# Contracting 128 rows instead of 64 in the products of a head's last key tile

## The chip, the cores and the metric

The kernel runs on one core of a Trainium2 chip. The metric is the device time of one execution in microseconds (us); of several executions the median is given. A profile is of one execution. TensorE (PE) multiplies: it loads a block of weights (PEld, up to 128 rows by 128 columns) and streams a moving operand through it; the rows are the ones that a product contracts. VectorE (DVE), ScalarE (ACT) and GpSimd (POOL) do the rest, SyncE (SP) issues most transfers. Each engine takes its instructions in order.

## The reference

64 heads (8 batches of 8) of causal attention with a decay, 576 positions of 64 values each, and then a two-layer network over the 4608 rows:

```python
scores = scale * np.matmul(q, k.transpose(0, 1, 3, 2))      # 64 heads, 576 x 576
cum = np.cumsum(np.log(np.clip(f, 0.0001, 1.0)), axis=-1)
scores = np.where(causal, -1000000000.0, scores + cum[:, :, :, None] - cum[:, :, None, :])
attn = np.exp(scores - np.max(scores, axis=-1, keepdims=True))
attn = attn / (np.sum(attn, axis=-1, keepdims=True) + 1e-09)
x = np.matmul(attn, v)                                      # -> 4608 x 512
h = np.maximum(x @ w_in, 0.0)                               # 512 -> 2048
out = h * h @ w_out                                         # 2048 -> 512
```

## The kernel before

Scores are computed transposed: keys lie on partitions and queries along the free axis, so that the exponentials `p` of a key tile are directly the moving operand of the product with V ("AV"). The 576 keys make five key tiles, four of 128 and a last one of 64 (`KT`; `kn` is a tile's number of keys). `UNITS` lists the six units of a head as (key tile, first query, end of queries): tile 0 for queries 256 to 576, tiles 2, 3, 4 and 1, and tile 0 for the queries below 256. Unit 3 is the last key tile: 64 keys by 64 queries. V comes from memory with 640 rows, of which the last 64 are zero.

There are two kinds of heads. The first 14 (`NWHOLE`, "whole" heads) use float32 as it is, which PE takes in two passes. In them the causal mask of a diagonal block is a product of its own behind the score product: the matrix `mz` (whose last 128 columns hold -1e9 above the diagonal) times a unit matrix `eye`, both bfloat16, accumulated on the scores (lines 346 and 348). Their AV is one product of V with `p` (line 411). The other 50 ("split" heads) split each operand into a high and a low part: two score products (lines 352 and 355), the exponential on ACT into `p` (362), the mask as an affine select on POOL (364), a cast of `p` to the high part `ph` on ACT (377), the low part `pl` by a subtraction on DVE (378), and three AV products, low times high, high times low, high times high (388, 389, 390), 65 columns of weights wide with a column of ones for the denominator (64 in the middle one).

The work is laid out in slots, one for each unit of each head. A slot emits the score and exponential of its unit (`score`), the AV products of the unit two slots back (`LAG`), and then what tables put there: loads, the preparation of later heads, row maxima (a product at line 313, a reduction on DVE at 319, a small transfer that writes the maxima into a row of the score's operand), and divisions. A split head's cast and subtraction follow in the next slot at the latest (`split_last`). In the first slots the weights are converted (DVE, ACT, and a subtraction on POOL at 210); when eight heads are done, the network's products (line 477 for the first layer, 500 for the second) fill in between (`fill`). The order of tracing is the order on PE, ACT, DVE and POOL (`in_order`); tile pools and semaphores do the rest. The buffers of `p` rotate: two in the split heads, three each for odd and even units in the whole heads (they share the names `ph` and `pl`).

Of the kernel before, what the change touches and what calls it, by code (L numbers as in the profile page):

```python
# [9 lines left out]
F32 = mybir.dt.float32  # L10
# [4 lines left out]
ALU = mybir.AluOpType  # L15
# [18 lines left out]
def decay_attention_relu2_kernel(  # L34
# [18 lines left out]
    nc = tc.nc  # L53

    NH, D, _, S = qk.shape
    P = 2 * D
    H = 8
    B = NH // H
    NJ = v.shape[2]
# [22 lines left out]
    def bank(use):  # L82

        turn = banks[use] or banks["s"]
        b = turn.pop(0)
        turn.append(b)
        return psum.tile([P, 512], F32, name=f"bank{b}")


    MW = 448  # L90
    mz = cpool.tile([P, MW], BF16, name="mz")
    nc.gpsimd.memset(mz, 0.0)
    nc.gpsimd.affine_select(
        out=mz[:, MW - P:], in_=mz[:, MW - P:], pattern=[[-1, P]],
# [3 lines left out]
    eye = wk.tile([P, 448], F32, name="p").bitcast(BF16)[:, :P]  # L98
    nc.gpsimd.memset(eye, 0.0)
    nc.gpsimd.affine_select(  # L100
        out=eye, in_=eye, pattern=[[-1, P]],
# [124 lines left out]
    KT = [(j * P, min(P, S - j * P)) for j in range(NJ)]  # L226
# [110 lines left out]
    def score(h, u):  # L337
        st = state[h]
        j, q0, q1 = UNITS[u]
        k0, kn = KT[j]  # L340
        n = q1 - q0
        ps = bank("s")
        if h < NWHOLE:
            masked = q0 == k0
            r, k = st["whole"][:, 0], st["whole"][:, 1]
            nc.tensor.matmul(ps[:kn, :n], k[:, k0:k0 + kn], r[:, q0:q1], start=True, stop=not masked)
            if masked:
                nc.tensor.matmul(
                    ps[:kn, :kn], mz[:kn, MW - P:MW - P + kn], eye[:kn, :kn], start=False, stop=True,
                )  # L350
        else:
            nc.tensor.matmul(  # L352
                ps[:kn, :n], st["kl0"][:D + 3, k0:k0 + kn], st["r2"][:D + 3, q0:q1], start=True, stop=False,
            )
            nc.tensor.matmul(  # L355
                ps[:kn, :n], st["l2"][:, k0:k0 + kn], st["r1"][:, q0:q1], start=False, stop=True,
            )
        if h < NWHOLE:
            p = wk.tile([P, 448], F32, name=("ph", "pl")[u % 2], bufs=3)
        else:  # L360
            p = wk.tile([P, 448], F32, name="p")
        nc.scalar.activation(out=p[:kn, :n], in_=ps[:kn, :n], func=AF.Exp, scale=SCALE)  # L362
        if h >= NWHOLE and q0 == k0:
            nc.gpsimd.affine_select(  # L364
                out=p[:kn, :kn], in_=p[:kn, :kn], pattern=[[1, kn]],
                compare_op=ALU.is_ge, fill=0.0, base=0, channel_multiplier=-1,
            )
        st["p"][u] = p

    def split_p(h, u):  # L370
        st = state[h]
        j, q0, q1 = UNITS[u]
        kn, n = KT[j][1], q1 - q0
        p = st["p"][u]
        ph = wk.tile([P, 448], F32R, name="ph", bufs=3)
        pl = wk.tile([P, 448], F32R, name="pl", bufs=3)
        nc.scalar.copy(out=ph[:kn, :n], in_=p[:kn, :n])  # L377
        nc.vector.tensor_tensor(  # L378
            out=pl[:kn, :n], in0=p[:kn, :n], in1=ph[:kn, :n].bitcast(F32), op=ALU.subtract,
        )  # L380
        st["p"][u] = ph, pl

    def av_split(st, acc, u, o, i, first, last):
        j = UNITS[u][0]
        kn = KT[j][1]
        ph, pl = st["p"][u]
        vh, vl = st["vh"][:kn, j, :D + 1], st["vl"][:kn, j, :]
        nc.tensor.matmul(acc[:D + 1, o], vh, pl[:kn, i], start=first, stop=False)  # L388
        nc.tensor.matmul(acc[:D, o], vl, ph[:kn, i], start=False, stop=False)  # L389
        nc.tensor.matmul(acc[:D + 1, o], vh, ph[:kn, i], start=False, stop=last)  # L390

    def av_part(h, u, low):

        j, q0, q1 = UNITS[u]
        s0, s1 = (q0, min(q1, QA)) if low else (max(q0, QA), q1)
        if s0 >= s1:
            return
        st = state[h]
        first = u == (NU - 1 if low else 0)
        last = u == NU - 2  # L400
        if first:
            st["av"] = bank("av")
        acc = st["av"]
        kn = KT[j][1]
        base = 0 if low else QA
        o, i = slice(s0 - base, s1 - base), slice(s0 - q0, s1 - q0)
        if h < NWHOLE:

            vr = st["vr"].rearrange("p j d -> p (j d)")
            vr = vr[:kn, j * (D + 2):min(j * (D + 2) + P, NJ * (D + 2))]  # L410
            nc.tensor.matmul(acc[:vr.shape[1], o], vr, st["p"][u][:kn, i], start=first, stop=last)
        else:
            av_split(st, acc, u, o, i, first, last)
        if last:
            n = QA if low else S - QA
            if not low:
                if h % H == 0:
                    xts[h // H] = wk.tile([P, NCC, S], F32, name=f"xt{h // H % 2}", bufs=1)
                if h % 2 == 0:
                    st["den"] = wk.tile([P, S], F32, name="den")  # L420
                else:
                    st["den"] = state[h - 1]["den"]
            o = (h % 2) * D
            x = xts[h // H][o:o + D, (h % H) // 2, base:base + n]
            nc.scalar.copy(out=x, in_=acc[:D, :n])
            nc.scalar.copy(out=st["den"][o:o + 1, base:base + n], in_=acc[D:D + 1, :n])  # L426
# [136 lines left out]
    def split_last():  # L563
        while unsplit:
            split_p(*unsplit.pop())
# [79 lines left out]
    for n in range(-2 * NU, last_slot + 1):  # L645
        live = 0 <= n < len(slots)
        split_last()
        if live:
            h, u = slots[n]
            score(h, u)  # L650
            if h >= NWHOLE:
                unsplit.append((h, u))
        for ha, ua in avs.get(n, ()):
            if ua < NU - 1:
                av_part(ha, ua, False)
            else:
                av_part(ha, ua, True)
                av_part(ha, ua - 1, True)
        for args in fins.get(n, ()):
            finish(*args)  # L660
        for do in events.get((n, 0), ()):
            do()
        wr = RATES[0 if n < -NU else 1 if n < 0 else 2 if n < NA else 3]
        cv(wr / 2)
        fill(n, 0.5)
        for do in events.get((n, 1), ()):
            do()
        cv(wr / 2)
        fill(n, 1.0)
# [44 lines left out]
```

## Time and profile before

| | |
|---|---|
| median of 3 runs | 1255.66 us (1254.82 to 1255.89) |
| the profiled execution | 1255.36 us |
| its span, first to last instruction | 1253.3 us |
| granted clock of PE, mean | 0.995 |
| busy: PE, PEld, DVE, ACT, POOL | 1193.5, 1051.8, 785.1, 702.0, 372.4 us |
| HBM read, written | 60.20, 9.88 MB |
| products of 64 rows: line 348, line 411, lines 388 to 390 | 14, 28, 3 x 50 |

Busy times overlap: a PE product counts from its start until its modelled end, and the next starts meanwhile. The distance between two starts tells what a product costs in a chain. In the rows, `64*65` behind a product is the number of rows and columns of its weights, and `64x64` the partitions and elements of the moving operand; float32 rows may stand for the rounded type too. An arrow `<-` behind a time names what ended the wait.

### The profile page before, as it was taken

What the parts mean: (1) busy time and instruction counts of PE and PEld (TensorE: products, weight loads), DVE (VectorE), ACT (ScalarE), POOL (GpSimd) and SP (SyncE); (2) the same over time, 40 slices, a digit from 0 to 9 for tenths busy, and PEclk for the clock granted to TensorE, in tenths of its full rate; (3) what the DMA queues carried; (4) which work ended last, traced back from release to release, by engine and by line L of the source; (5) the groups of instructions that cost most, each with busy time, mean ns of one, the idle gap of its engine ahead of it and who ended that gap; (6) DMA issues with size and microseconds to landing.
All of it is one profiled execution on the core that took longest, in us unless ns stands there. A gap on an engine that the chain in (4) does not pass through costs nothing.

```text
span 1253.3 us, 23182 instructions
## 1 busy us (share of the span) xinstructions
PE 1193.5 (95%) x7652; PEld 1051.8 (84%) x7652; DVE 785.1 (63%) x2042; ACT 702.0 (56%) x1720; POOL 372.4 (30%) x512
## 2 busy tenths in 40 slices
PE   3877899999999999999999999999999999999998
PEld 2544687888989899999899989998998989999997
DVE  7658776666666767666656566667665766532332
ACT  3545455556666666665565556666666666632332
POOL 4323223333333333333322233334333333200000
PEclk9999999999999999999999999999999999999999
DMA  8857631112121112121201121211121212000000
GB/s 199 193 129 176 177 87 26 51 32 57 41 55 33 48 37 57 40 57 26 55 18 52 31 57 32 55 34 52 40 57 41 57 41 52 17 27 1 18 18 17
DMA packets 115639, 71.90 MB, mean 57 GB/s; under 512 B 97384, under 2 KB 97384, under 8 KB 115520
## 3 DMA queue, kind: packets, MB, share of 16 engines
q1 hardware_dynamic: 114400, 66.30, 21.7%
q0 software_dynamic: 1120, 4.13, 1.5%
q8 instruction: 61, 1.00, 0.3%
q14 instruction: 58, 0.48, 0.1%
HBM read 60.20 MB, written 9.88 MB: 56 GB/s over the span
## 4 chain that ended last, share of the span: by engine, by line
PE 63%; ACT 1%; issue 1%; POOL 1%; DMA 0%; DVE 0%; SPq 0%; POOLq 0%; DVEq 0%; ACTq 0%
PE bank L477 25%; PE bank L500 24%; PE bank L388 3%; PE bank L355 2%; PE bank L390 2%; PE bank L389 2%; PE bank L313 2%; PE bank L352 2%; DMA den<-rdr 0%; ACT ph L377 0%; ACT den L426 0%; ACT r L485 0%; ACT p L362 0%; POOL v L299 0%; ACT rl L281 0%
## 5 line engine op out<-in xcount | busy, mean ns | idle before, releaser
L500 PE MATMUL bank<-w,gh 128*128 128x512 f32 x1152 | 413.8, 400 | 0.0
L477 PE MATMUL bank<-xh,w 128*128 128x256 f32 x2304 | 330.7, 286 | 4.9 <-DVE tcol L319 4.9
L378 DVE TENSOR_TENSOR pl<-p,ph 128x320 fp32r<-128x320 f32 (+4 forms) x300 | 186.9, 623 | 206.6 <-ACT ph L377 197.1
L477 PEld LDWEIGHTS bank<-xh,w 128*128 128x128 f32 x2304 | 301.2, 190 | 13.8 <-DVE tcol L319 5.3
L500 PEld LDWEIGHTS bank<-w,gh 128*128 128x128 f32 x1152 | 217.6, 189 | 39.0
L485 ACT ACTIVATE r<-bank 128x256 f32<-128x256 f32 x288 | 110.4, 383 | 211.7 <-PE bank L477 198.3
L500 PE MATMUL bank<-w,gl 128*128 128x512 f32 x576 | 227.1, 394 | 0.2 <-DVE gl L488 0.2
L486 DVE TENSOR_TENSOR g<-r 128x256 f32<-128x256 f32 x288 | 127.3, 442 | 144.2 <-ACT r L485 143.4
L364 POOL TENSOR_SCALAR_AFFINE_SELECT p<-p 128x128 f32<-128x128 f32 (+1 forms) x250 | 81.5, 326 | 454.2 <-ACT p L362 313.5
L377 ACT CAST ph<-p 128x320 fp32r<-128x320 f32 (+4 forms) x300 | 124.4, 415 | 148.9 <-POOL p L364 147.1
L477 PE MATMUL bank<-xl,w 128*128 128x256 f32 x1152 | 185.3, 283 | 0.0
L319 DVE CUSTOM_DVE_ANT_0 bank<-bank,mz 128x256 f32<-128x256 f32 (+4 forms) x320 | 133.7, 432 | 45.9 <-PE bank L313 44.5
L477 PEld LDWEIGHTS bank<-xl,w 128*128 128x128 f32 x1152 | 158.9, 191 | 0.0
L362 ACT ACTIVATE p<-bank 128x320 f32<-128x320 f32 (+4 forms) x300 | 115.8, 386 | 71.7 <-PE bank L355 67.3
L488 DVE TENSOR_TENSOR gl<-g,gh 128x256 fp32r<-128x256 f32 x288 | 128.9, 448 | 35.7 <-ACT p L362 0.9
L313 PE MATMUL bank<-rk 66*128 66x320 f32 (+9 forms) x384 | 111.8, 318 | 24.8 <-DMA rk<-qkraw 13.4
L487 ACT ACTIVATE gh<-r 128x256 fp32r<-128x256 f32 x288 | 120.5, 418 | 9.1
L500 PEld LDWEIGHTS bank<-w,gl 128*128 128x128 f32 x576 | 109.3, 190 | 14.3 <-DVE gl L488 0.9
L313 PEld LDWEIGHTS bank<-rk 66*128 66x128 f32 (+3 forms) x384 | 68.7, 185 | 40.1 <-DVE tcol L319 17.1
L388 PE MATMUL bank<-pl,vh 128*65 128x320 f32 (+4 forms) x350 | 99.4, 284 | 1.6 <-ACT den L426 1.4
L389 PE MATMUL bank<-ph,v 128*64 128x320 f32 (+4 forms) x350 | 94.8, 271 | 0.0
L390 PE MATMUL bank<-ph,vh 128*65 128x320 f32 (+4 forms) x350 | 93.0, 271 | 0.0
(71 smaller groups left out, 1498.2 us busy)
## 6 DMA issues: line engine op xcount, KB each, us to landing
qkraw<-in_qk SPq DMA_DIRECT2D x50, 288.0 KB
v<-in_v SPq DMA_DIRECT2D x64, 160.0 KB
den<-rdr SPq DMA_DIRECT2D x64, 144.0 KB
out<-osb SPq DMA_DIRECT2D x36, 256.0 KB
w<-in_w_in SPq DMA_DIRECT2D x16, 512.0 KB
w<-in_w_out SPq DMA_DIRECT2D x16, 512.0 KB
rl<-in_qk SPq DMA_DIRECT2D x14, 288.0 KB
rk<-in_qk POOLq DMA_DIRECT2D x14, 288.0 KB, 4.7
```

What stands on the lines that cost most here:

```text
L313: nc.tensor.matmul(ps[:m, :n], st["r2"][:rows, q0:q0 + m], st["kl0"][:rows, k0:k0 + n], start=True, stop=True,)
L319: nc.vector.tensor_tensor_reduce(out=ps[:m, :n], in0=ps[:m, :n], in1=mz[:m, mo:mo + n], op0=ALU.add, op1=ALU.min, scale=-1.0, scalar=init, ...
L377: nc.scalar.copy(out=ph[:kn, :n], in_=p[:kn, :n])
L378: nc.vector.tensor_tensor(out=pl[:kn, :n], in0=p[:kn, :n], in1=ph[:kn, :n].bitcast(F32), op=ALU.subtract,)
L388: nc.tensor.matmul(acc[:D + 1, o], vh, pl[:kn, i], start=first, stop=False)
L389: nc.tensor.matmul(acc[:D, o], vl, ph[:kn, i], start=False, stop=False)
L390: nc.tensor.matmul(acc[:D + 1, o], vh, ph[:kn, i], start=False, stop=last)
L477: nc.tensor.matmul(ph[:, :T], w[:, s, cc], x[:, cc, :], start=(cc == 0 and k == 0), stop=(cc == NCC - 1 and k == 2),)
L486: nc.vector.tensor_tensor(out=g, in0=r, in1=r, op=ALU.mult)
L487: nc.scalar.activation(out=gh, in_=r, func=AF.Square)
L488: nc.vector.tensor_tensor(out=gl, in0=g, in1=gh.bitcast(F32), op=ALU.subtract)
L500: nc.tensor.matmul(po, g[:, ts], w[:, s], start=(fc == 0 and k == 0), stop=(fc == NF - 1 and k == 2),)
```

## The change

Where the last key tile's operands have 64 partitions, the change uses all 128. The mask product takes all rows of `mz` and `eye`, whose rows 64 to 127 are zero in the columns used. Partitions 64 to 127 of the exponentials' buffer are cleared on POOL, while the exponential goes on writing 0 to 63; the cast and the subtraction run over all 128 partitions; and the AV products contract 128 rows, in which the rows of keys that don't exist are zero in `p`, `ph`, `pl` and V. Units of full key tiles are as before, and the score products keep their shape.

```diff
-                    ps[:kn, :kn], mz[:kn, MW - P:MW - P + kn], eye[:kn, :kn], start=False, stop=True,
+                    ps[:kn, :kn], mz[:, MW - P:MW - P + kn], eye[:, :kn], start=False, stop=True,
...
+        if kn < P:
+
+            nc.gpsimd.memset(p[kn:, :n], 0.0)
         nc.scalar.activation(out=p[:kn, :n], in_=ps[:kn, :n], func=AF.Exp, scale=SCALE)
...
-        nc.scalar.copy(out=ph[:kn, :n], in_=p[:kn, :n])
+        nc.scalar.copy(out=ph[:, :n], in_=p[:, :n])
         nc.vector.tensor_tensor(
-            out=pl[:kn, :n], in0=p[:kn, :n], in1=ph[:kn, :n].bitcast(F32), op=ALU.subtract,
+            out=pl[:, :n], in0=p[:, :n], in1=ph[:, :n].bitcast(F32), op=ALU.subtract,
         )
...
-        vh, vl = st["vh"][:kn, j, :D + 1], st["vl"][:kn, j, :]
-        nc.tensor.matmul(acc[:D + 1, o], vh, pl[:kn, i], start=first, stop=False)
-        nc.tensor.matmul(acc[:D, o], vl, ph[:kn, i], start=False, stop=False)
-        nc.tensor.matmul(acc[:D + 1, o], vh, ph[:kn, i], start=False, stop=last)
+        vh, vl = st["vh"][:, j, :D + 1], st["vl"][:, j, :]
+        nc.tensor.matmul(acc[:D + 1, o], vh, pl[:, i], start=first, stop=False)
+        nc.tensor.matmul(acc[:D, o], vl, ph[:, i], start=False, stop=False)
+        nc.tensor.matmul(acc[:D + 1, o], vh, ph[:, i], start=False, stop=last)
...
-            vr = vr[:kn, j * (D + 2):min(j * (D + 2) + P, NJ * (D + 2))]
-            nc.tensor.matmul(acc[:vr.shape[1], o], vr, st["p"][u][:kn, i], start=first, stop=last)
+            vr = vr[:, j * (D + 2):min(j * (D + 2) + P, NJ * (D + 2))]
+            nc.tensor.matmul(acc[:vr.shape[1], o], vr, st["p"][u][:, i], start=first, stop=last)
```

On PE, ACT and DVE no instruction is added or moved; PE's keep their order, and only the row counts change, which the listed order does not tell. On POOL 64 memsets come in. In a split head it stands ahead of the affine select of the same tile. POOL before, in the middle of the split heads (brackets: the engines and queues whose semaphores an instruction waits for):

```order
L364 AFFINE_SELECT p<-p 128x128 [waits Activation_49]
L364 AFFINE_SELECT p<-p 64x64 [waits Activation_49]
L290 TENSOR_TENSOR rl<-qkraw,rl 64x576 [waits Pool_49]
L364 AFFINE_SELECT p<-p 128x128 [waits DVE_49,Activation_49,Pool_49]
L299 TENSOR_TENSOR v<-v,vh_80 128x320 [waits DMAHW7_49,DVE_49,PE_49]
```

And with the change (three lines came in above, so that line 364 is now the memset and 367 the select):

```order
L367 AFFINE_SELECT p<-p 128x128 [waits Activation_49]
L364 MEMSET p 64x64 [waits DVE_49,Pool_49]
L367 AFFINE_SELECT p<-p 64x64 [waits Activation_49]
L290 TENSOR_TENSOR rl<-qkraw,rl 64x576
L367 AFFINE_SELECT p<-p 128x128 [waits DVE_49,Activation_49,Pool_49]
```

One instruction came in, with a wait for DVE, which reads the buffer's earlier content; the rest kept its order. In a whole head the memset stands behind POOL's part in the weights (`w`, line 210) and ahead of a later head's load (252). POOL with the change, in the first whole heads:

```order
L268 MEMSET v 128x5x2
L210 TENSOR_TENSOR w_250<-osb,w_250 128x512 [waits DMAHW6_49,Activation_49]
L364 MEMSET pl 64x64 [waits Pool_49]
L252 DMA rk_77<-in_qk 64x1152 [waits DMASW1_49,PE_49]
L210 TENSOR_TENSOR w_302<-osb,w_302 128x512 [waits DMAHW7_49,Activation_49,Pool_49]
```

On ACT the exponential of the last tile in the whole heads (from the second head on) waits for POOL too. Before:

```order
L426 COPY den<-bank_309 1x256
L362 ACTIVATE ph<-bank_323 128x192 [waits PE_49,Activation_49]
L181 ACTIVATE wmag<-w_193 128x512 [waits DMAHW0_49,DVE_49]
L362 ACTIVATE pl<-bank_345 64x64 [waits PE_49,Activation_49]
L362 ACTIVATE ph<-bank_354 128x448 [waits PE_49,Activation_49]
```

And with the change:

```order
L427 COPY den<-bank_310 1x256
L365 ACTIVATE ph<-bank_324 128x192 [waits PE_49,Activation_49]
L181 ACTIVATE wmag<-w_193 128x512 [waits DMAHW0_49,DVE_49]
L365 ACTIVATE pl<-bank_346 64x64 [waits PE_49,Activation_49,Pool_49]
L365 ACTIVATE ph<-bank_356 128x448 [waits PE_49,Activation_49]
```

Nothing moved there; the fourth row has one wait more. In the split heads the exponential has no such wait.

More of the change, by code (lines that the diff above doesn't have):

```diff
@@ L372, in split_p @@
         j, q0, q1 = UNITS[u]
-        kn, n = KT[j][1], q1 - q0
+        n = q1 - q0
         p = st["p"][u]
@@ L384, in av_split @@
         j = UNITS[u][0]
-        kn = KT[j][1]
         ph, pl = st["p"][u]
-        vh, vl = st["vh"][:kn, j, :D + 1], st["vl"][:kn, j, :]
-        nc.tensor.matmul(acc[:D + 1, o], vh, pl[:kn, i], start=first, stop=False)
-        nc.tensor.matmul(acc[:D, o], vl, ph[:kn, i], start=False, stop=False)
-        nc.tensor.matmul(acc[:D + 1, o], vh, ph[:kn, i], start=False, stop=last)
+        vh, vl = st["vh"][:, j, :D + 1], st["vl"][:, j, :]
+        nc.tensor.matmul(acc[:D + 1, o], vh, pl[:, i], start=first, stop=False)
+        nc.tensor.matmul(acc[:D, o], vl, ph[:, i], start=False, stop=False)
+        nc.tensor.matmul(acc[:D + 1, o], vh, ph[:, i], start=False, stop=last)
     def av_part(h, u, low):
@@ L403, in av_part @@
         acc = st["av"]
-        kn = KT[j][1]
         base = 0 if low else QA
```

## The prediction

> **What bounds the kernel now.** I began with the head of the page, then asked for the busy time of each engine by stage.
>
> ```profile
> span 1253.3 us, 23182 instructions
> PE 1193.5 (95%) x7652; PEld 1051.8 (84%) x7652; DVE 785.1 (63%) x2042; ACT 702.0 (56%) x1720; POOL 372.4 (30%) x512
> ```
>
> ```profile
> 31.00:62.00 31.00, 25.28 (x124) 17.71 (x123) 19.11 (x57) 18.15 (x45) 9.89 (x14) 1.00 0.84 194
> 125.00:157.00 32.00, 26.17 (x137) 20.99 (x136) 24.03 (x49) 14.56 (x35) 8.85 (x11) 0.91 0.65 175
> 157.00:188.00 31.00, 30.35 (x182) 25.19 (x181) 22.95 (x57) 16.02 (x39) 8.17 (x8) 1.00 0.33 87
> ...
> 220.00:1110.00 890.00, 884.05 (x5917) 798.34 (x5916) 584.89 (x1562) 548.98 (x1367) 300.31 (x423) 1.00 0.18 44
> ```
>
> The columns are the stretch, its length, and the busy time (with instruction count) of PE, PEld, DVE, ACT and POOL, then granted clock, DMA share and GB/s. There are two regimes. Up to about 157 us PE is busy for only 25 to 26 us of each 31 or 32 while the DMA engines are 65 to 84% busy: loads and the conversion of the weights hold the pace. From there on PE is busy almost without a break, 884.05 of 890 us in the stretch that holds the 50 split heads, with the clock at 1.00. No other engine is above 66% there. The waits of PE in that stretch, longest first, confirm it:
>
> ```profile
> PE bank L313 <- DVE tcol L319: 3.4, 3, 1.6
> PE bank L388 <- ACT den L426: 1.4, 4, 0.4
> ```
>
> The longest wait group is 3.4 us in 890. So in this stretch what PE spends is what the kernel spends, and a busy PE is not yet a PE at its peak: a product's recorded time includes its latency. What a product costs is the distance from its start to the next start, and that is in the timeline. Here is PE around the last key tile's three AV products of one split head (columns: start, duration, engine, line, operation and tiles, rows*columns of the weights, shape of the moving operand):
>
> ```profile
> 578.92 0.28 PE L355 MATMUL bank<-rl 128*128 128x256 f32 x1
> 579.13 0.24 PE L388 MATMUL bank<-pl,vh 64*65 64x64 f32 x1
> 579.21 0.22 PE L389 MATMUL bank<-ph,v 64*64 64x64 f32 x1
> 579.27 0.22 PE L390 MATMUL bank<-ph,vh 64*65 64x64 f32 x1
> ...
> 580.47 0.40 PE L477 MATMUL bank<-xl,w 128*128 128x256 f32 x2
> ```
>
> And the same lines for a full key tile, in the same head's neighbourhood, contracting 128 rows and followed by the same MLP products:
>
> ```profile
> 586.43 0.28 PE L390 MATMUL bank<-ph,vh 128*65 128x256 f32 x1
> 586.55 0.22 PE L388 MATMUL bank<-pl,vh 128*65 128x128 f32 x1
> 586.61 0.22 PE L389 MATMUL bank<-ph,v 128*64 128x128 f32 x1
> 586.67 0.22 PE L390 MATMUL bank<-ph,vh 128*65 128x128 f32 x1
> ...
> 587.73 0.64 PE L477 MATMUL bank<-xl,w 128*128 128x256 f32 x4
> ```
>
> A product with a 256-wide moving operand passes on after 0.12 us (586.43 to 586.55), but before the 64-row product 0.21 us go by (578.92 to 579.13): 0.09 us lost on entry. From the last product of the trio to the first xl product of the MLP take 1.06 us with 128 rows (586.67 to 587.73) and 1.20 us with 64 rows (579.27 to 580.47), though the latter moves half as many columns: 0.14 us lost on exit. So the path into and out of a 64-row product is not pipelined. Is it the rows, or that everything here is 64 wide? This kernel has narrow products with more than 64 rows:
>
> ```profile
> 593.50 0.20 PE L352 MATMUL bank<-rk 67*64 67x64 f32 x1
> 593.53 0.22 PE L355 MATMUL bank<-rl 128*64 128x64 f32 x1
> 593.59 0.34 PE L388 MATMUL bank<-pl,vh 128*65 128x320 f32 x1
> ...
> 597.82 0.20 PE L313 MATMUL bank<-rk 66*64 66x64 f32 x1
> ...
> 598.88 0.64 PE L477 MATMUL bank<-xl,w 128*128 128x256 f32 x4
> ```
>
> With 64 columns of weights and 64 moving columns, but 67 and 128 rows, the steps are 0.03 and 0.06 us, and from a 66-row one to the xl product again 1.06 us (597.82 to 598.88). Rows of 66 or 67 lose nothing, rows of 64 do. The gap belongs to the contraction of 64 rows.
>
> **The change part by part.**
>
> *AV of the last tile, split heads.* Three products per head go from 64 to 128 rows; their number and their moving columns stay.
>
> ```profile
> L388 PE MATMUL bank<-pl,vh 64*65 64x64 f32 x50 | 12.1, 242 | 0.0
> ```
>
> Fifty heads, one trio each. Before, from the start of the product ahead to the first xl product: 580.47 - 578.92 = 1.55 us. After, two bounds. By the 128-wide trio: 0.12 + 0.06 + 0.06 + 1.06 = 1.30 us, saving 0.25. By the narrow products at their shortest step: 0.12 + 0.03 + 0.03 + 1.06 = 1.24 us, saving 0.31. The second narrow product above is already followed after 0.06 us, as though the next weights set the step, so I stay close to the first: 0.26 us, 50 x 0.26 = 13.0 us. Should one of the two ends keep its gap, about 0.1 to 0.15 us a head would be left; nothing in the 128-row rows speaks for that. A loss on PE is excluded by the same rows: no product of these lines with 128 rows starts later than its neighbour's columns ask.
>
> The Trainium skill's page "TensorE: Matmul & The Clock Gate", section "Why this matters for your kernels", says that a single product with 32 rows takes the same time as one with 128. By that rule every term on PE would be zero and the kernel's time 1255.4 us; the rows above, 1.20 us against 1.06 us behind products of 64 and 66 rows, disagree for products in a chain with others.
>
> *Mask product and AV in the 14 whole heads.* Here the mask product contracts 64 rows and then 128, and the AV product (two passes) likewise:
>
> ```profile
> 98.56 0.33 PE L346 MATMUL bank<-rl 128*64 128x64 f32 x2
> 98.82 0.21 PE L348 MATMUL bank<-p,mz 64*64 64x64 bf16 x1
> 98.96 0.81 PE L411 MATMUL bank<-pl,v 128*128 128x320 f32 x2
> ...
> 100.35 0.22 PE L348 MATMUL bank<-p,mz 128*128 128x128 bf16 x1
> 100.41 0.54 PE L411 MATMUL bank<-ph,v 128*128 128x192 f32 x2
> ...
> 101.22 0.22 PE L348 MATMUL bank<-p,mz 128*128 128x128 bf16 x1
> 101.37 0.33 PE L411 MATMUL bank<-pl,v 64*66 64x64 f32 x2
> ```
>
> A 128-row mask passes on after 0.06 us (100.35 to 100.41); a 64-row mask after 0.14 (98.82 to 98.96), and into a 64-row AV product it takes 0.15 (101.22 to 101.37). So an end costs 0.08 to 0.09 us again, and each of the two 64-row places of a whole head has two ends: some 0.2 us for each, 0.4 us a head (estimate, from the split trio's 0.23 at its two ends). Whether that counts depends on the regime.
>
> ```profile
> L348 PE MATMUL bank<-p,mz 64*64 64x64 bf16 x3 | 0.6, 213 | 0.0
> ```
>
> Three such masks lie between 157 and 220 us, where PE is the bound: 3 x 0.4 = 1.2 us. The other 11 heads are worth 11 x 0.4 = 4.4 us on PE, in a stage where PE idles a fifth of the time. Both ends are open: nothing, if loads and weights alone hold the pace, or all of it, if the idle time only follows PE's own order. PE's idle share there is near the first, so I take a quarter: 1.1 us.
>
> *The added memset.* POOL clears 64x64 values 64 times. Nearest rows:
>
> ```profile
> L268 POOL MEMSET v<- 128x10 f32 x14 | 1.8, 125 | 0.0
> L117 POOL MEMSET rl<- 64x576 f32 x2 | 1.1, 574 | 0.1
> ```
>
> Ten values per partition cost 125 ns, 576 cost 574; interpolated, 64 cost about 170 ns, with these two as ends. 64 of them are 11 us of POOL, which is 30% busy. In a split head the memset stands between two affine selects on POOL, and what it could delay is the second one (behind the exponential of the same tile), then the cast and the subtraction, then the AV products two slots on. Around one:
>
> ```profile
> 568.51 0.29 POOL L364 TENSOR_SCALAR_AFFINE_SELECT p<-p 128x128 f32<-128x128 f32 x1 [1.93 <-ACT p L362]
> 571.79 0.22 ACT L362 ACTIVATE p<-bank 64x64 f32<-64x64 f32 x1 [0.82 <-PE bank L355]
> ```
>
> POOL is free at 568.80 and the exponential starts only at 571.79, because PE's scores come late: 3 us of cover for 0.17 us. The memset's wait for the buffer's last reader (DVE) is one that the exponential has already. I put it at nothing; without the cover it would delay one tile's select by 0.17 us. In the whole heads the exponential itself gains a wait for the memset (13 of 14), and there POOL can be late:
>
> ```profile
> 98.59 1.27 POOL L210 TENSOR_TENSOR w<-osb,w 128x512 fp32r<-128x512 f32 x1 [5.33 <-ACT w L209]
> 99.80 0.11 POOL L268 MEMSET v<- 128x10 f32 x1
> 99.13 0.22 ACT L362 ACTIVATE pl<-bank 64x64 f32<-64x64 f32 x1 [0.61 <-PE bank L348]
> 100.75 0.68 ACT L181 ACTIVATE wmag<-w 128x512 f32<-128x512 f32 x1 [1.40 <-DVE osb L197]
> ```
>
> Here the memset could start at 99.91 and the exponential at about 100.1 instead of 99.13, 0.95 us late. It would end by 100.3, ahead of its reader at 101.37, and ACT's next work comes at 100.75. Behind the memset POOL's queue holds the load of a later head, which would go out 0.17 us later. Cost: nothing here, and zero to 1 us over the stage; I take zero.
>
> *The wider cast and subtraction* work on 128 partitions instead of 64 with the same 64 columns. Elements per partition don't change; no price.
>
> *What is late next.* DVE and ACT have a third of their time free, so a head that is 0.26 us shorter (of some 17.8: 890 us over 50 heads) leaves them cover; still, some small waits will grow where PE arrives earlier. I take back 5% of 13.0, 0.6 us.
>
> Sum: 13.0 + 1.2 + 1.1 - 0.6 = 14.7 us. The profiled execution took 1255.36 us (span 1253.3), 0.3 us below the median of 1255.66. 1255.36 - 14.7 = 1240.7 against its own time; against the median 1241.0.
>
> **The rivals.**
>
> *The time is given back as waits.* Each product of the next head needs maxima from DVE and a bank that ACT has emptied, and the two wait rows above show that PE already touches both. If half of the 13.0 us turned into such waits, and the early heads gave nothing, the time would be 1255.7 - 6.5 - 0.6 = 1248.6 us. Against it: those waits total under 5 us now and the engines are at two thirds. 1 in 10.
>
> *The early heads give all.* If PE's order holds the first stage as well, 4.4 us come instead of 1.1, and with 0.31 us a trio the time would be 1255.7 - 15.5 - 1.2 - 4.4 = 1234.6 us. PE's 25 of 31 us leave it possible: 1 in 12.
>
> *No change.* If the gap comes from something that these 64-column products share and rows don't touch, 1255.7 us. The 66- and 67-row products speak against it: 3 in 100. The page's rule named above would end here too.
>
> *Slower: ACT behind POOL in the whole heads.* The new wait makes ACT, which issues in order, stand behind POOL's weight subtractions (L210, 1.27 us) when it comes to the last tile's exponential. If all 13 heads lost 1.27 + 0.17 = 1.4 us and all of that reached PE, 18.7 us would be lost against 14.7 won: 1259.7 us. It decides from about 1.1 us a head reaching PE. In the case above 0.95 us would arise and be absorbed. 3 in 100.
>
> **How the numbers follow.** The forecast holds 3 of 4 chances, 1241.0 us. Its own range runs from 1255.7 - 15.5 - 1.2 - 2 = 1237 to 1255.7 - 12.5 + 1.8 = 1245 (0.25 us a head, nothing from the early heads, 1.8 us of new waits or of ACT's delay). The range for 8 in 10 reaches into the two neighbouring rivals, 1236 to 1247; outside lie no change, slower, and the far parts of these two. A measurement of this kernel can tell 0.2% (2.5 us) from no change. All but no change and slower make it faster by more than that: faster 0.93, same 0.04, slower 0.03 (a little of the first rival's tail goes to same).
>
> **What would show it.** In the timeline after, the trio should start 0.12 us behind the score product, step by 0.03 to 0.06, and the distance from its first neighbour to the first xl product should be 1.24 to 1.30 us in place of 1.55. The split heads' stretch should shrink by 12 to 15 us, the stretch before 157 us by at most 4. POOL should show 64 memsets near 170 ns, with no exponential waiting on POOL in the split heads. PE's waits for DVE and ACT should stay under 8 us between 220 us and the last head. The prediction is wrong if the 128-row trio keeps either gap, if PE's idle time grows by about what the gaps gave, or if ACT's waits for POOL in the whole heads appear as PE idle time.

## The result, and the profile after

| | before | changed |
|---|---|---|
| median of 4 runs | 1255.24 us (1254.28 to 1255.89) | 1242.68 us (1241.21 to 1245.07) |
| ratio | | 0.9902, 95% interval 0.9879 to 0.9925 |
| the profiled execution | 1255.36 us | 1241.21 us |

Faster by 12.6 us; 14.7 were forecast, as 1241.0 us in 1236 to 1247. Run again beside the experiments, twice, the changed kernel stood at 0.9905 (0.9886 to 0.9924) and 0.9897 (0.9878 to 0.9916). The first rows to read are again the stretches of the changed kernel (length, then busy time of PE, PEld, DVE, ACT and POOL, clock, DMA share, GB/s):

```profile
31.00:62.00 31.00, 24.07 (x123) 17.12 (x121) 18.80 (x56) 17.83 (x44) 10.55 (x17) 1.00 0.85 181
125.00:157.00 32.00, 27.45 (x149) 22.93 (x148) 23.91 (x51) 14.90 (x36) 8.80 (x10) 0.86 0.61 164
220.00:1110.00 890.00, 882.97 (x5994) 804.12 (x5993) 589.64 (x1576) 551.84 (x1375) 308.25 (x472) 1.00 0.18 44
```

Busy time hardly tells of the change: PE's 882.97 us of 890 were 884.05 before. What has changed is how many products fit in, 5994 for 5917. The distances in the timeline of the changed kernel tell why (start, duration, engine, line, weights as rows*columns, moving operand):

```profile
571.85 0.28 PE L355 MATMUL bank<-rl 128*128 128x256 f32 x1
571.97 0.19 PE L390 MATMUL bank<-pl,vh 128*65 128x64 f32 x1
572.00 0.22 PE L391 MATMUL bank<-ph,v 128*64 128x64 f32 x1
572.06 0.22 PE L392 MATMUL bank<-ph,vh 128*65 128x64 f32 x1
572.12 1.20 PE L478 MATMUL bank<-xh,w 128*128 128x256 f32 x8
573.15 0.40 PE L478 MATMUL bank<-xl,w 128*128 128x256 f32 x2
```

The first of the trio now starts 0.12 us behind the score product (0.21 before), the next ones after 0.03 and 0.06, and the xl product comes at 1.30 us (1.55 before). Over 49 heads the median of that distance fell from 1553 to 1300 ns. The whole heads show it too:

```profile
98.43 0.33 PE L346 MATMUL bank<-rl 128*64 128x64 f32 x2
98.59 0.19 PE L348 MATMUL bank<-p,mz 128*64 128x64 bf16 x1
98.71 0.81 PE L412 MATMUL bank<-pl,v 128*128 128x320 f32 x2
...
100.98 0.22 PE L348 MATMUL bank<-p,mz 128*128 128x128 bf16 x1
101.03 0.28 PE L412 MATMUL bank<-pl,v 128*66 128x64 f32 x2
```

From the narrow score pair to its AV neighbour take 0.28 us (0.40 before), and into the last tile's AV product 0.05 (0.15 before). The clearing on POOL, and the exponential that it had to precede:

```profile
L364 POOL MEMSET p<- 64x64 f32 x50 | 7.3, 147 | 5.0 <-DVE pl L381 2.3
L364 POOL MEMSET pl<- 64x64 f32 x14 | 3.8, 270 | 0.8
...
561.79 0.15 POOL L364 MEMSET p<- 64x64 f32 x1
564.72 0.22 ACT L365 ACTIVATE p<-bank 64x64 f32<-64x64 f32 x1 [0.82 <-PE bank L355]
```

147 ns in the split heads, 270 in the whole ones, and done 2.8 us before the exponential starts. Last, the waits of PE between 220 and 1110 us:

```profile
PE bank L313 <- DVE tcol L319: 3.6, 3, 1.7
PE bank L390 <- ACT den L427: 2.3, 7, 0.4
PE bank L313 <- DVE rk L280: 0.7, 2, 0.4
```

The wait for ACT's copy of the denominator, line 427, has grown from 1.4 to 2.3 us. That is part of what is missing from the forecast; the experiments look for the rest.

### The profile page after: what moved, and what is told of

Its sections match the earlier page's. It is cut to its first block, busy times and chain, and to the rows that moved or that the text cites. A ratio compares the mean times of both kernels' runs of the same rounds, so it can differ in the third digit from the quotient of the medians.

```text
span 1239.5 us, 23297 instructions
## 1 busy us (share of the span) xinstructions
PE 1179.0 (95%) x7652; PEld 1047.0 (84%) x7652; DVE 785.6 (63%) x2042; ACT 701.3 (57%) x1720; POOL 383.4 (31%) x576
## 4 chain that ended last, share of the span: by engine, by line
PE 62%; ACT 2%; issue 2%; POOL 1%; DMA 0%; DVE 0%; SPq 0%; POOLq 0%; DVEq 0%; ACTq 0%
PE bank L478 25%; PE bank L501 24%; PE bank L390 3%; PE bank L313 2%; PE bank L355 2%; PE bank L392 2%; PE bank L391 2%; PE bank L352 2%; DMA den<-rdr 0%; ACT r L486 0%; ACT den L427 0%; ACT p L365 0%; ACT ph L380 0%; ACT rl L281 0%; POOL xt L448 0%
## 5 line engine op out<-in xcount | busy, mean ns | idle before, releaser
L390 PE MATMUL bank<-pl,vh 128*65 128x320 f32 (+4 forms) x350 | 96.9, 277 | 2.3 <-ACT den L427 2.3
```

What stands on the lines that cost most here:

```text
L390: nc.tensor.matmul(acc[:D + 1, o], vh, pl[:, i], start=first, stop=False)
```

## The experiments

My theory: the loss sits where PE passes between products of 64 rows and products of more, a fixed amount for each passage; the rest of the kernel has slack enough to let most of it through. The rivals: the saving comes from the whole heads or is eaten by ACT's new wait for POOL there; each 64-row product costs a fixed amount; the full array is what counts, not the step over 64; the clearing costs something. Every experiment ran beside the kernel before, and the ratios are to it.

**Where the 12 us come from: each part alone.** The first kernel leaves the whole heads as before:

```diff
-        if kn < P:
+        if kn < P and h >= NWHOLE:
             nc.gpsimd.memset(p[kn:, :n], 0.0)
# mask product and AV product of the whole heads: rows [:kn] as before
```

> Only the 50 split heads are changed (clearing, cast, subtraction and AV products over 128 rows); the mask and AV products of the 14 whole heads stay at 64 rows. Theory (the 64-row trio loses 0.25 us a head on the path of PE): 50 x 0.25 = 12.5 us, about 1242.8 us, a ratio of 0.990. Rival (the saving in the split heads is partly given back as waits, and part of the 12.6 us of the whole change came from the whole heads): 1245 us or more.

Measured: 1245.43 us, ratio 0.9925 (0.9904 to 0.9947), by the ratio 9.4 us faster (0.0075 x 1255). The trio saves its 253 ns a head here as well, and yet the time is the rival's: the theory's 12.5 us (0.990) lie just outside the interval. The second leaves the split heads as before:

```diff
-        if kn < P:
+        if kn < P and h < NWHOLE:
             nc.gpsimd.memset(p[kn:, :n], 0.0)
# cast, subtraction and AV products of the split heads: rows [:kn] as before
```

> Only the 14 whole heads are changed (clearing, mask product and AV product over 128 rows); the split heads stay at 64 rows. Theory (loads and weights pace the first stage, PE only its end): the first split trio comes 1 to 2 us earlier, 1253.5 to 1254.5 us. Rival 1 (PE's order holds the first stage too): 14 x 0.4 = 5.6 us, about 1249.7 us. Rival 2 (ACT behind POOL costs what PE gains): 1255.3 us or above.

Measured: 1252.62 us, ratio 0.9972 (0.9956 to 0.9988), 1.5 to 5.5 us faster. So the split heads give some 9.4 us, the whole heads some 3, and both together the change. The theory's 0.7 to 1.7 us reach only into the near end of the interval, and rival 1's 5.6 us lies just beyond its far end: the first stage seems to follow PE's order in part. Rival 2 is out.

**Does the clearing cost anything?**

```diff
-        nc.tensor.matmul(acc[:D + 1, o], vh, pl[:, i], start=first, stop=False)
+        nc.tensor.matmul(acc[:D + 1, o], vh[:kn], pl[:kn, i], start=first, stop=False)
# and so in all products; clearing, cast and subtraction stay at 128 partitions
```

> The clearing on POOL and the cast and subtraction over 128 partitions as in the changed kernel, but all products contract 64 rows as before. If the clearing is hidden, it equals the kernel before, 1255.2 us within 2 us; if ACT's wait for POOL costs in the whole heads, it is slower by 2 to 10 us.

Measured: 1253.86 us, ratio 0.9986 (0.9971 to 1.0002). It costs nothing that can be seen. The wait that it puts before the exponentials of the whole heads was taken away by itself:

```diff
+    pads = [et[:, D + i * D:D + (i + 1) * D] for i in range(2)]   # free columns of the tile that holds eye
+    for x in pads:
+        nc.gpsimd.memset(x[D:], 0.0)
...
+        if h < NWHOLE and kn < P:
+            p = pads[h % 2]
```

> The whole change, but the whole heads' last-tile exponentials go to two fixed buffers whose partitions 64 to 127 are cleared once at the start, so no exponential of a whole head waits for POOL; the split heads clear each time as in the changed kernel. If the wait of ACT for POOL eats part of the whole heads' gain, this is 1 to 4 us faster than the changed kernel, 1239 to 1241.5 us, with the first split trio before 230 us; if loads and weights pace that stage, it equals the changed kernel within 1 us, about 1242.5 us.

Measured: 1244.25 us, ratio 0.9909 (0.9888 to 0.9931), the same as the changed kernel beside it, 1243.81:

> The changed kernel itself, beside the others on the same chip: 1242.7 us again, ratio 0.990. The four runs so far spread over 3.9 us where the kernel before spreads over 1.6; if that comes from how often PE's clock is halved in the first 157 us, runs with a lower mean clock are the longer ones.

ACT's wait for POOL costs nothing that can be told. On the clock, single profiles say little: the changed kernel's with a mean clock of 0.996 has a span of 1237.8 us, its shortest, 1236.5 us, has 0.992. But over the 51 executions of the kernel before that ran beside the experiments, those with a lower mean clock are the longer ones, by some 0.7 us for each thousandth of the clock (correlation -0.62; -0.55 in 16 executions of the changed kernel). So the clock accounts for part of the spread, and not for all of it.

**Passages or products?** In its split heads, the next kernel has fewer 64-row products than the kernel before and twice as many passages (with the clearing and the cast over 128 partitions that this takes):

```diff
# against the changed kernel, split heads; the whole heads are as in the kernel before
-        nc.tensor.matmul(acc[:D + 1, o], vh, pl[:, i], start=first, stop=False)
-        nc.tensor.matmul(acc[:D, o], vl, ph[:, i], start=False, stop=False)
-        nc.tensor.matmul(acc[:D + 1, o], vh, ph[:, i], start=False, stop=last)
+        nc.tensor.matmul(acc[:D + 1, o], vh[:kn], pl[:kn, i], start=first, stop=False)
+        nc.tensor.matmul(acc[:D, o], vl[:P], ph[:P, i], start=False, stop=False)
+        nc.tensor.matmul(acc[:D + 1, o], vh[:kn], ph[:kn, i], start=False, stop=last)
```

> The kernel before with one difference in the split heads: the middle one of the three AV products of the last key tile contracts 128 rows (cleared partitions, cast over 128), the first and third stay at 64, so a head crosses between 64 and 128 rows four times instead of twice, with two 64-row products instead of three. If each crossing costs about 0.11 us, the stretch from the score product to the first xl product grows from 1.55 to about 1.75 to 1.8 us and the kernel is 10 to 12 us slower than before, about 1266 us. If each 64-row product costs a fixed amount by itself (0.08 us each), it is a third less loss, about 1251 us.

Measured: 1264.53 us, ratio 1.0073 (1.005 to 1.0096). Slower by some 9 us, where passages ask for 10 to 12; the 1251 us of a cost for each product are out. Its timeline:

```profile
583.32 0.28 PE L355 MATMUL bank<-rl 128*128 128x256 f32 x1
583.53 0.24 PE L391 MATMUL bank<-pl,vh 64*65 64x64 f32 x1
583.70 0.24 PE L392 MATMUL bank<-ph,v 128*64 128x64 f32 x1
583.88 0.24 PE L393 MATMUL bank<-ph,vh 64*65 64x64 f32 x1
584.05 1.21 PE L480 MATMUL bank<-xh,w 128*128 128x256 f32 x8
585.10 0.52 PE L480 MATMUL bank<-xl,w 128*128 128x256 f32 x3
```

Every product of the trio stands 0.17 to 0.21 us from its neighbours, where the 128-row trio steps by 0.03 and 0.06. The median from score product to xl product is 1779 ns: four passages cost 1779 - 1300 = 479 ns, 120 each; the two of the kernel before cost 1553 - 1300 = 253 ns, 127 each.

The weight loads show what differs at a passage. Here are the load ahead of the trio and the load behind it, first before (the trio begins at 579.13 us and the network's products at 579.42 us), then with the change (571.97 and 572.12 us):

```profile
579.13 0.13 PEld L388 LDWEIGHTS bank<-pl,vh 64*65 64x65 f32 x1
579.41 1.01 PEld L477 LDWEIGHTS bank<-xh,w 128*128 128x128 f32 x8
...
571.86 0.14 PEld L390 LDWEIGHTS bank<-pl,vh 128*65 128x65 f32 x1
572.09 1.02 PEld L478 LDWEIGHTS bank<-xh,w 128*128 128x128 f32 x8
```

With the change the loads run ahead of their products, in the median of 50 heads by 115 and 28 ns; at the two passages of the kernel before, and at all four of the last kernel, a load starts 1 to 2 ns ahead of its product. Between two 64-row products it runs ahead as usual (26 ns). What holds it back at a passage no run here shows.

**64 rows or less than all?**

```diff
-            nc.gpsimd.memset(p[kn:, :n], 0.0)
+            nc.gpsimd.memset(p[kn:66, :n], 0.0)
# and rows [:66] in place of [:] in mask, cast, subtraction and AV
```

> The whole change with 66 rows instead of 128 (two cleared partitions instead of 64), in mask, AV, cast and subtraction. If the gap belongs to 64 rows or fewer, this equals the changed kernel: 1.30 us from score product to xl product, about 1243.5 us, ratio 0.990. If the full array is what counts, or the gap shrinks with the rows missing, it stays near the kernel before, 1253 to 1255 us.

Measured: 1243.29 us, ratio 0.9898 (0.9877 to 0.9919). Its trio:

```profile
573.40 0.28 PE L355 MATMUL bank<-rl 128*128 128x256 f32 x1
573.52 0.20 PE L392 MATMUL bank<-pl,vh 66*65 66x64 f32 x1
573.55 0.22 PE L393 MATMUL bank<-ph,v 66*64 66x64 f32 x1
...
574.70 0.28 PE L481 MATMUL bank<-xl,w 128*128 128x256 f32 x1
```

The step into the trio is 0.12 us, within it 0.03, and the first xl product (the row shows that one alone) comes at 1.30 us. Over 49 heads the median to the first xl product is 1293 ns. Two rows more than 64 do all that 64 rows more do.

**Where the rest went.** I laid the distances between neighbouring starts, summed by kind over the split heads, of the changed kernel beside those of the kernel with changed whole heads only. The trio's own kinds, and the products right behind it, shrink by 12.1 us. Two kinds grow in every kernel with the 128-row or 66-row trio in which the AV bank and its copies are as before: from a score product of 192 columns to the next head's first AV product (11.3 us in 49 heads with 64 rows, 12.0 with 128), and from an AV product to the network's first layer (7.3, then 8.1). Ahead of the maxima at line 313 it is from nothing up to 1.3 us more, differing by the profile. The first of these is PE waiting for the one accumulator bank of AV; most of its growth comes from three heads, of which this is one, in the changed kernel

```profile
489.87 0.27 PE L355 MATMUL bank<-rl 128*128 128x192 f32 x1
490.40 0.36 PE L390 MATMUL bank<-pl,vh 128*65 128x320 f32 x1 [0.26 <-ACT den L427]
```

and the same head with the 64-row trio (line 392 is the same product):

```profile
494.90 0.27 PE L355 MATMUL bank<-rl 128*128 128x192 f32 x1
495.18 0.36 PE L392 MATMUL bank<-pl,vh 128*65 128x320 f32 x1
```

0.53 us for 0.28. The second kind grows in four places of 50, at which there was no wait before, from 0.15 us to 0.34. One of them, with ACT's read of a network bank that ends 0.05 us ahead of the product:

```profile
725.06 0.38 ACT L486 ACTIVATE r<-bank 128x256 f32<-128x256 f32 x1
...
725.15 0.30 PE L392 MATMUL bank<-ph,vh 128*65 128x320 f32 x1
725.49 1.21 PE L478 MATMUL bank<-xh,w 128*128 128x256 f32 x8
```

Two kernels tried to take the first wait away. The first has a second accumulator bank, paid for with a score bank:

```diff
-                    banks.update(s=[1, 2, 3, 5], o0=[6], o1=[7])
+                    banks.update(s=[1, 2, 3], av=[0, 5], o0=[6], o1=[7])
```

> The changed kernel, with two accumulator banks for AV in turn instead of one from the third chunk of the network on (and three instead of four for scores and maxima). With one bank PE stands before a head's first AV product until ACT has copied the last one's denominator, some 0.1 us a head, 12.0 us over the split heads from score to AV where 90 ns apiece would be 4.5. If that wait is the bank, this is 4 to 7 us faster than the changed kernel, about 1238 us; if the missing score bank costs as much, the same; if the wait is ACT's whole backlog, it only moves to the next product.

Measured: 1248.8 us, ratio 0.995 (0.993 to 0.997). That is slower than the changed kernel (0.9905 and 0.9897), which none of the three expectations had. The wait went, 12.0 us shrinking to 5.7, so it is the bank. But now PE waits for the maxima, which share the score banks:

```profile
PE bank L313 <- DVE tcol L319: 7.2, 9, 1.6
PE bank L313 <- DVE rk L280: 1.7, 3, 0.7
```

In the changed kernel the same two waits are 3.6 and 0.7 us. The distances into the products of the maxima grow to 54.0 us, from 45.2 to 46.3 in three profiles of the changed kernel, and those out of them to 36.9 from 30.4. The stretch from first to last split trio, 855.8 us, is some 6 us longer than the changed kernel's. The second kernel copies the denominator on DVE:

```diff
-            nc.scalar.copy(out=st["den"][o:o + 1, base:base + n], in_=acc[D:D + 1, :n])
+            if low and h >= NWHOLE:
+                nc.vector.tensor_copy(out=st["den"][o:o + 1, base:base + n], in_=acc[D:D + 1, :n])
+            else:
+                nc.scalar.copy(out=st["den"][o:o + 1, base:base + n], in_=acc[D:D + 1, :n])
```

> The changed kernel, with the denominator row of the low accumulator copied by DVE instead of ACT in the split heads, so that the two copies that free the one AV bank run side by side (0.36 us each on ACT before). If PE's wait before a head's first AV product, 12.0 us over the split heads, is for that bank, some 5 us of it go and the kernel is 3 to 5 us faster than the changed one, about 1239.5 us. If DVE's queue comes to the copy later than ACT did, the wait stays or grows, 1243 to 1247 us.

Measured: 1260.24 us, ratio 1.006 (1.0038 to 1.0081).

```profile
PE bank L390 <- DVE den L428: 13.7, 14, 2.5
```

DVE comes to the copy much later than ACT, and the wait it was to shorten grew from 2.3 us to 13.7; the kernel is slower by far than the 1243 to 1247 us that were expected for this case. Part of that is the clock: four of the waits last some 2.5 us, and within 1.5 us behind three of them PE's clock is halved for 3.4 us, which is some 5 us in all (estimate, half of 3 x 3.4). Neither beats the changed kernel, which ran a third time beside it:

> The changed kernel beside it on the same chip: 1243.3 us, ratio 0.990.

Measured: 1240.44 us, ratio 0.9897 (0.9878 to 0.9916).

## Why the prediction was right, point by point

*PE as the bound from 157 us on:* right. What the trio saves on PE moves the end.

*The trio:* 0.26 us a head forecast, 0.253 measured, and 12.4 us over the 49 heads between the first and the last trio. The choice of the upper bound of time (1.30 us) against the lower (1.24) was right, but its terms were not: one step within the trio is 0.03 us where 0.06 stood, and the way out is 1.09 us where 1.06 stood. That the two balance is luck. The cause, 64 rows against more, is shown by the 66-row kernel, and that it is the passage, by the kernel with four of them. The Trainium skill, "TensorE: Matmul & The Clock Gate", section "Why this matters for your kernels", says that a single product with 32 rows takes as long as one with 128. Carried over to these products, that would have made all of this nothing; the measurement, 1553 ns against 1300, decides against it for products among others with more rows.

*Given back as waits:* 0.6 us forecast, and this is the term that was mis-sized. From the first split trio to the last, profiles of kernels with the 64-row trio and no drop of PE's clock in that stretch need 859.8 and 860.2 us (the kernels with whole heads only and with clearing only); the changed kernel needs 849.5, 850.2 and 849.7 in three profiles. That is 10.2 us less, not 12.4 (and not the 12 to 15 by which this stretch was to shrink): some 2.2 us went back. 0.7 of them stand at the AV bank and its copies on ACT, 0.8 ahead of the network's first layer, where ACT's read of a bank ends the wait in the places that grew; the rest differs from profile to profile, and its cause stays open. I had named waits for DVE and for banks that ACT empties, in the first rival too, and put them at 5%; they were 18%. As I read it, the mistake was to judge their room by how busy ACT and DVE are on average, 62 and 66%, when PE already stood at the bank in 38 of 49 heads (11.3 us from score to AV, of which two banks leave 5.7). The kernel with four passages shows the same trade the other way: its trios cost 11.1 us more, its stretch (868.8 us) only 8.8, and the distances at the bank shrank from 11.3 us to 10.1.

The two profiled executions differ by 14.15 us, and flatter the change: in that of before PE's clock was halved for 3.4 us near 281 us, which cost some 1.7 us there (861.7 us for the stretch against 859.8 and 860.2).

*The whole heads:* 2.3 us forecast (1.2 late, 1.1 early), 1.5 to 5.5 measured. The mask place saved 0.12 us where 0.2 stood: the way into it gave 0.09 (0.15 to 0.06), the way out only 0.02 (0.14 to 0.12, where a wide mask passes on after 0.06), and why is not shown. The AV place gave 0.09 on the way in and 0.05 between its two passes (0.11 to 0.06); its way out can't be told apart from the waits behind it. The first split trio starts at 231.1 us in the mean of eight profiles with 128 or 66 rows in the whole heads, and at 233.8 in four with 64, with 6 us between the ends of the first group: the sum is about right, and not known better, and how it divides into late and early heads is not shown.

*The clearing, the cast and the subtraction:* nothing, as forecast; 147 ns for 170 in the split heads. In the whole heads it took 270 ns, and that didn't matter. In the profile no exponential keeps ACT idle for POOL, and PE's waits for the other engines between 220 and 1110 us come to 6.8 us, within the 8 forecast.

The sum by what was measured: 12.4 - 2.2 + 2.7 = 12.9 us, beside the 12.6 of the medians.

## What to carry to other kernels

On a chain of products that keeps TensorE busy, look at the distance from start to start, not at busy time: in this kernel, products of 64 rows among ones with more cost 0.12 us at each passage, and with zero rows added, two of them already, that cost was gone. When something on the bound gets shorter, look at each place where it needs another engine in a round: some of the gain comes back there, at places where it already waits a little and at places where it just doesn't, whatever the mean load of the engine waited for. A wait that is removed at the price of another shared buffer, or by handing the work to an engine further behind, may cost more than it held.

## What was not expected of the hardware

That the full array is not needed: 66 rows do what 128 do (1293 and 1300 ns), as the prediction had read from two narrow products; and that columns don't matter: with 128 rows, the middle product's weights have 64 columns between neighbours with 65, and in the trio of a full key tile every step is 0.06 us. That at a passage the weight load no longer runs ahead of its product. That PE's clock was halved right behind three of four waits of some 2.5 us. And that the start varies so much: the first split trio comes at 227.8 to 231.1 us in three profiles of the changed kernel, while the tail behind the last trio took 158.9 to 159.3 us in every profile. The kernel before ran between 1248.0 and 1261.5 us over all its executions here.
